# Short matmuls sent one by one between the long ones in a planned Trainium2 kernel

## The chip, the cores and the metric

The kernel runs on one core of a Trainium2 chip. The metric is the device time of one execution in microseconds (us). A core has TensorE (PE; its weight loads are shown apart as PEld), VectorE (DVE), ScalarE (ACT), GpSimd (POOL) and the DMA queues that SyncE (SP) and GpSimd issue to. Each engine works through its own list of instructions in order, and engines wait for each other on semaphores.

## The reference

The input `A_x` has 2048 rows of 512 numbers. Two branches are computed from it and mixed by a gate for each row:

```python
def reference(A_x, A_w_r, A_w_i, B_x, B_w1, B_b1, B_w2, B_b2, gate_w):
    # X = rfft2(x); X = X * (w_r + 1j * w_i); a = irfft2(X)          (spectral filter)
    # b = gelu(x @ w1 + b1) @ w2 + b2                                 (512 -> 1792 -> 512)
    g = _sigmoid((x * gate_w).sum(-1, keepdims=True))
    a = _A_ref(x, A_w_r, A_w_i)
    b = _B_ref(x, B_w1, B_b1, B_w2, B_b2)
    return g * a + (1 - g) * b
```

Everything is in 32-bit floats. Both branches are given the same `x`.

## The kernel before

**Tiling.** The 2048 rows are 16 blocks of 128, and four groups (c = 0 to 3) of four blocks make the 512 columns of one matmul in the dense branch. Matmuls take operands rounded to a shorter mantissa, so each operand is split into a high and a low part and a product is made of three: high x high, high x low, low x high (`prods`, line 533).

**The dense branch** is `mlp(half, c)`: 14 slices of the hidden width in two halves, four groups each. For a slice, `up` (line 1087) makes the tile `ph` by twelve matmuls of 512 columns (four slices of the input, three products each); ACT applies the gelu, and `split` makes its high part on ACT and its low part on DVE (`g_...`). Then `down` adds three matmuls of 512 columns for each slice into the tiles `po`. The last `po` is made in two pieces of 256 columns.

**The spectral branch** has a forward part, `forward(j)`, for each of the 16 blocks: DVE folds the block, and the step at line 736 makes, for each of two products c, two matmuls of 260 columns from the high part (`pd<-cf,eoh`); the step at line 737 adds two of 130 columns from the low part (`pd<-cf,eol`). ACT (lines 739, 740) and DVE (742, 743) read `pd`, three matmuls of 512 columns make `py`, and ACT and DVE put it into `y`. Then come butterflies on `y` and the filter, all on DVE, and the way back, `inverse(c, h)`: for each of two blocks, `pz` is made by two matmuls of 256 columns from the high part (`some(vh, 0, True)`) and, in the step `rest` (line 971), two of 128 from the low part, two of 256 and again two of 128; ACT (line 979) and DVE (980) read `pz`. Twelve matmuls of 256 columns make `pa`.

**The order of the work** is not the order of the code. Each call of `m`, `a`, `v`, `dma` and so on adds a step to a graph (`Graph.add`), with an engine, a cost, a lag from its end until others may use its result, the buffers that it reads and writes, and a rank. `Graph.schedule` then plays the engines through: whenever one is free by its clock, it takes the ready step with the lowest rank for which buffers are free. Ranks come from the list `RANKS`, one number for each step. The plan's order is the order in which instructions are emitted, for all engines and DMA queues. For TensorE the cost is given by `c_pe` (line 495), with a floor for short matmuls:

```python
    def c_pe(n, k=1):
        return k * max(n / 2400 + 0.0135, 0.112)
```

that is, n columns at 2400 a microsecond and 0.0135 us, but not under 0.112 us, for each of k matmuls. All matmuls are issued by the helper `mm`, so they have line 531 in the profile and are told apart by tile.

Of the kernel before, what the change touches and what calls it, by code (L numbers as in the profile page):

```python
# [17 lines left out]
P = 128  # L18
NJ = S // P
NF = F // P  # L20
NQ = D // P
# [6 lines left out]
NC = P + 2  # L28
# [132 lines left out]
class Step:  # L161
    def __init__(self, n, eng, cost, lag, emit, bufs, rank):
        self.n, self.eng, self.cost, self.lag, self.emit, self.bufs, self.rank = n, eng, cost, lag, emit, bufs, rank
        self.after = []
        self.need = 0

        self.open = 0
        self.there = 0.0
        self.table = None
        self.at = None  # L170


class Graph:
# [47 lines left out]
    def schedule(self):  # L221
# [11 lines left out]
        wire = 0.0  # L233
        events = []
# [32 lines left out]
        while True:  # L267
            for e in list(ready):
                while ready[e] and busy.get(e, 0.0) <= now:
                    kept, got = [], None  # L270
                    while ready[e]:
                        r = heapq.heappop(ready[e])
                        new = takes(r[2])
                        if new is None or held(e, r[2]):
                            kept.append(r)
                            continue
                        got = r[2]
                        break
                    for r in kept:
                        heapq.heappush(ready[e], r)  # L280
                    if got is None:
                        break
                    s = got
                    for b in new:
                        b.slot = free[b.tag].pop(0)
                        held_by[b.cls] += 1
                        nxt[b.cls] += 1
# [6 lines left out]
                    if e in ("sp", "pool"):  # L294
                        busy[e] = now + (0.5 if e == "sp" else 0.95)
                        wire = max(wire, now) + s.cost
                        end = wire + s.lag
                    else:
                        busy[e] = now + cost
                        end = now + cost + s.lag  # L300
                    for q in s.after:
# [990 lines left out]
```

## Time and profile before

| what | value |
|---|---|
| median of 3 runs | 373.58 us (373.31 to 374.03) |
| the profiled execution's own time | 372.75 us |
| its span, first to last instruction | 370.6 us |
| granted TensorE clock | 0.999 |
| matmuls | 1790: 1370 of 512 columns, 292 of 256 to 260, 64 of 130, 64 of 128 |
| DVE busy | 326.6 us |
| ACT busy | 234.5 us |

The profile is of one execution. Its page has busy times by engine, the same by slices of the span, and the chain that ended last; other views give waits, groups of instructions by line or tile, busy time in stretches, and the instructions in order of time. In a timeline row the columns are the start in us, the length in us, the engine, the line, the operation, output tile <- input tiles, shapes, and how many were merged into the row ("x2"). Matmuls overlap in the array: the length of one runs from its entry to the end of its results, so two lengths cover the same time in part, and distances between starts say how fast TensorE goes. A matmul and its weight load are separate instructions; the load (PEld) of a matmul stands ahead of it.

### The profile page before, as it was taken

The numbers are of one execution on the slowest core, as the hardware profiler recorded it, in microseconds if no ns is written. First come the engines' busy times: TensorE is split into PE (matmuls) and PEld (weight loads), VectorE is DVE, ScalarE is ACT, GpSimd is POOL, SyncE is SP. The second block draws the span as 40 slices with busy tenths as digits, with TensorE's granted clock in tenths as the row PEclk, the third lists the DMA queues.
The fourth block names the chain that finished last, engine by engine and source line by source line (L and its number), as shares of the span: only waits on it lengthen the run. The fifth ranks groups of instructions, "written<-read, shape, count | busy, mean of one in ns | idle before, by whom it ended". The sixth has DMA issues, their size and how long they took to land.

```text
span 370.6 us, 5520 instructions
## 1 busy us (share of the span) xinstructions
PE 364.5 (98%) x1790; PEld 307.4 (83%) x1790; DVE 326.6 (88%) x689; ACT 234.5 (63%) x462; POOL 44.1 (12%) x54
## 2 busy tenths in 40 slices
PE   7999999999999999999999999999999999999995
PEld 6888888888888888888888788888888888888895
DVE  5999889999999779899998999878749895989996
ACT  6768697886679655355366313697497649647820
POOL 0000000000000002021023011000332123111041
PEclk9999999999999999999999999999999999999999
DMA  8952889324953205587489792308996999824368
GB/s 278 381 184 72 287 297 356 105 86 145 309 167 112 84 22 146 144 197 172 140 191 243 130 259 42 73 0 309 183 142 124 182 286 239 142 73 99 114 88 197
DMA packets 39628, 62.99 MB, mean 170 GB/s; under 512 B 4656, under 2 KB 17008, under 8 KB 38832
## 3 DMA queue, kind: packets, MB, share of 16 engines
q1 hardware_dynamic: 32256, 49.54, 40.6%
q0 software_dynamic: 7200, 12.85, 23.7%
q8 instruction: 14, 0.23, 0.3%
q10 hardware_dynamic: 144, 0.26, 0.2%
q14 instruction: 14, 0.11, 0.1%
HBM read 38.64 MB, written 23.73 MB: 168 GB/s over the span
## 4 chain that ended last, share of the span: by engine, by line
PE 76%; DVE 14%; DMA 6%; issue 2%; ACT 1%; SPq 0%
PE ph L531 32%; PE po L531 31%; DMA wf<-in_wf 5%; PE pz L531 4%; PE pd L531 4%; PE pa L531 3%; PE py L531 3%; DVE m L911 2%; DMA xr<-in_xt 1%; DVE y L811 1%; DVE y L813 1%; DVE y L815 1%; ACT mxh L655 0%; DVE y L915 0%; DVE y L913 0%
## 5 line engine op out<-in xcount | busy, mean ns | idle before, releaser
L1108 ACT ACTIVATE ph<-ph,b1t 128x512 f32<-128x512 f32 x56 | 36.8, 658 | 55.2 <-PE ph L531 55.1
L952 ACT ACTIVATE sw<-y,al 64x512 f32<-64x512 f32 x32 | 22.9, 721 | 3.1 <-DVE y L815 2.0
L959 DVE SCALAR_TENSOR_TENSOR pq<-y,al,sw 128x256 f32<-128x256 f32 x32 | 14.3, 481 | 8.5 <-ACT sw L955 7.8
L911 DVE TENSOR_TENSOR m<-y,wf 128x514 f32<-128x514 f32 x32 | 20.9, 690 | 0.2
L522 POOL DMA_DIRECT2D bacc<-o x12 | 11.2, 972 | 64.7 <-ACT o L1157 64.7
L522 POOL DMA_DIRECT2D wa7l<-in_w x1 | 1.0, 1015 | 142.9 <-ACT wa7l L583 142.9
L1154 ACT ACTIVATE o<-po,b2t 128x512 f32<-128x512 f32 x16 | 10.8, 687 | 9.1 <-PE po L531 9.1
L765 ACT ACTIVATE y<-py 64x256 f32<-64x256 f32 x32 | 12.1, 379 | 3.7 <-PE py L531 3.1
L1157 ACT ACTIVATE o<-po 128x512 f32<-128x512 f32 x12 | 6.9, 594 | 10.5 <-PE po L531 10.5
L531 PEld LDWEIGHTS pd<-cf,eoh 128*128 128x128 f32 x64 | 10.9, 188 | 2.1 <-ACT eoh L710 0.5
L1005 DVE TENSOR_TENSOR uv<-pa,od 128x512 f32<-128x512 f32 x16 | 10.5, 686 | 2.3 <-ACT od L1002 2.1
L531 PE MATMUL pd<-cf,eoh 128*128 128x260 f32 x64 | 12.4, 288 | 0.1
L762 ACT ACTIVATE y<-py 64x256 f32<-64x256 f32 x32 | 12.1, 378 | 0.5
L694 DVE TENSOR_TENSOR eo<-xr 128x256 f32<-128x256 f32 x30 | 11.7, 420 | 0.0
L1049 DVE SCALAR_TENSOR_TENSOR ba<-gb,ba 128x512 f32<-128x512 f32 x12 | 8.3, 688 | 2.8 <-DMA ba<-bacc 2.7
L531 PE MATMUL pd<-cf,eol 128*128 128x130 f32 x64 | 10.5, 251 | 0.0
L531 PEld LDWEIGHTS pd<-cf,eol 128*128 128x128 f32 x64 | 10.0, 188 | 0.3
L1002 ACT ACTIVATE od<-pa 128x512 f32<-128x512 f32 x8 | 4.8, 598 | 8.5 <-PE pa L531 8.5
L955 ACT ACTIVATE sw<-y 1x512 f32<-1x512 f32 x16 | 10.0, 628 | 0.3
L708 DVE TENSOR_TENSOR xr<-eo 128x256 f32<-128x256 f32 x24 | 9.7, 421 | 0.2
L522 POOL DMA_DIRECT2D out<-ba x8 | 7.3, 909 | 20.6 <-DVE ba L1049 10.3
L655 ACT ACTIVATE mxh<-xm 128x512 fp32r<-128x512 f32 x12 | 7.1, 629 | 3.6 <-PE ph L531 3.6
(713 smaller groups left out, 1337.3 us busy)
## 6 DMA issues: line engine op xcount, KB each, us to landing
wf<-in_wf SPq DMA_DIRECT2D x16, 257.0 KB, 3.7
bacc<-o SPq DMA_DIRECT2D x16, 256.0 KB, 4.7
xr<-in_xt SPq DMA_DIRECT2D x15, 256.0 KB, 4.1
war<-in_w SPq DMA_DIRECT2D x14, 256.0 KB, 3.9
wbr<-in_w SPq DMA_DIRECT2D x14, 256.0 KB, 4.1
xm<-in_xt SPq DMA_DIRECT2D x12, 256.0 KB, 4.9
bacc<-o POOLq DMA_DIRECT2D x12, 256.0 KB, 4.5
ba<-bacc SPq DMA_DIRECT2D x12, 256.0 KB, 4.0
```

The lines of the kernel that those rows point to most:

```text
L522: return add("pool", kb / 150, 3.4, lambda: nc.gpsimd.dma_start(dst(), src(), accum_op=ALU.add), reads, writes, rank)
L531: pe.matmul(ps, w, x, start=start, stop=stop)
L694: v(lambda s=s, op=op: vec.tensor_tensor(eo.ap()[:, s], x.ap()[:, 0:2], x.ap()[:, 2:4], op=op), 256, [x], [(eo, s)], FEED)
L762: a(lambda o=o, i=i: act.activation(apart(0, o, HP), py.ap()[i:i + HP, 1].rearrange("p (a b) -> p a b", a=2), AF.Copy), HD, [py], [(Y[j], ...
L765: a(lambda o=o, i=i: act.activation(Y[j].ap()[o:o + HP, 1, :HD], py.ap()[i:i + HP, 0], AF.Copy, scale=-1.0), HD, [py], [(Y[j], 1 + k)], 0, ...
L911: v(lambda mk=mk, k=k, y=y, w=w: vec.tensor_tensor(mk.ap(), y.ap()[:, :, :ND], w.ap()[:, k:k + 1, :ND].to_broadcast([P, 2, ND]), op=ALU.mu ...
L952: a(lambda sw=sw, y=y, o=o, i=i: act.activation(sw.ap()[o:o + HP], y.ap()[i:i + HP, ::-1, :HD], AF.Copy, scale=al.ap()[i:i + HP, 0:1]), 51 ...
L955: a(lambda sw=sw, y=y, j=j: act.activation(sw.ap()[HP:HP + 1], y.ap()[HP:HP + 1, ::-1, :HD], AF.Copy, scale=math.cos(math.pi * j / NJ)), 5 ...
L959: v(lambda sw=sw, pq_=pq_, y=y, j=j, k=k, op=op: vec.scalar_tensor_tensor(pq_.ap()[:, k], y.ap()[:, k, :HD], al.ap()[:, 1 + j:2 + j], sw.a ...
L1005: v(lambda i=i, op=op: vec.tensor_tensor(uv.ap()[:, :, i], ps.ap()[:, 0], od.ap(), op=op), 512, [ps, od], [(uv, i)], 2)
L1108: a(lambda f=f, ps=ps: act.activation(ps.ap(), ps.ap(), AF.Gelu_apprx_tanh, bias=b1t.ap()[:, f:f + 1]), 600, [b1t], [ps], 0.9 if half else ...
L1154: a(lambda o=o, ps=ps, q=q: act.activation(o.ap(), ps.ap(), AF.Identity, scale=-1.0, bias=b2t.ap()[:, q:q + 1]), 600, [b2t, ps], [o])
```

## The change

Steps of at most 130 columns (the low parts of `pd` and `pz`) are marked "short", those of 512 columns "long". When the plan is turned into instructions, the matmuls of a short step are held back. If the next step on TensorE is long, its matmuls and the held ones are issued in turn: one held, one long, one held, one long, and the rest of the long ones. Held ones are issued by themselves when a step of any engine is due at or after the time at which the plan counts their result as there, or when the next TensorE step is neither short nor long. The planner takes, after a short step, a ready long one ahead of lower ranks. It counts a short matmul without the floor, and the lag of a short step is longer by the cost of one long matmul for each matmul after the first. `up` becomes four steps of three matmuls, and the second step of `pz` three steps of two. There are 2040 ranks in place of 1843, all of them new. The matmuls themselves are the same.

```diff
@@ Graph.schedule
-                    kept, got = [], None
-                    while ready[e]:
-                        r = heapq.heappop(ready[e])
-                        new = takes(r[2])
...
+                    got = None
+                    for kind in ("long", None) if e == "pe" and last == "short" else (None,):
+                        kept = []
+                        while ready[e]:
+                            r = heapq.heappop(ready[e])
+                            if kind and r[2].kind != kind:
+                                kept.append(r)
+                                continue
+                            new = takes(r[2])
+                            if new is None or held(e, r[2]):
+                                kept.append(r)
+                                continue
+                            got = r[2]
+                            break
...
                     s = got
+                    if e == "pe":
+                        last = s.kind
...
+                    s.end = end
@@ tile_kernel
     def c_pe(n, k=1):
-        return k * max(n / 2400 + 0.0135, 0.112)
+        return k * (n / 2400 + 0.0135)
...
     def m(emit, n, k, reads, writes, rank=BULK):
-        return add("pe", c_pe(n, k), 0.25, emit, reads, writes, rank)
+        if n > P + 2:
+            s = add("pe", c_pe(n, k), 0.25, emit, reads, writes, rank)
+            s.kind = "long" if n == 4 * P else None
+        else:
+            s = add("pe", k * (n / 2400 + 0.0135), 0.25 + (k - 1) * c_pe(4 * P), emit, reads, writes, rank)
+            s.kind = "short"
+        return s
...
+    now = []
+
     def mm(ps, w, x, start, stop):
-        pe.matmul(ps, w, x, start=start, stop=stop)
+        now.append(lambda: pe.matmul(ps, w, x, start=start, stop=stop))
@@ forward
-            m(lambda c=c: prod(c, l, NC, False), 240, 2, [l, *cf_of(c)], [pd[c]], 0)
+            m(lambda c=c: prod(c, l, NC, False), NC, 2, [l, *cf_of(c)], [pd[c]], 0)
@@ inverse
             m(lambda some=some, vh=vh: some(vh, 0, True), 256, 2, [t, vh], [ps], FEED)
-            m(rest, 256, 6, [t, vh, vl], [ps], FEED)
+            m(lambda some=some, vl=vl: some(vl, 0, False), P, 2, [t, vl], [ps], FEED)
+            m(lambda some=some, vh=vh: some(vh, 1, True), 256, 2, [t, vh], [ps], FEED)
+            m(lambda some=some, vl=vl: some(vl, 1, False), P, 2, [t, vl], [ps], FEED)
@@ mlp
-                m(up, 512, 12, [*W["a", f], *xx], [ps])
+                for q in range(NQ):
+                    m(lambda up=up, q=q: up(q), 512, 3, [*W["a", f], *xx], [ps])
@@ the end of tile_kernel
     with tc.manual_schedule():
+        held = []
+        until = 0.0
+
+        def flush(between):
+            out = []
+            for k in range(max(len(held), len(between))):
+                out += held[k:k + 1] + between[k:k + 1]
+            for f in out:
+                f()
+            held.clear()
+
         for s in order:
+            if held and (s.at >= until or s.eng == "pe" and s.kind is None):
+                flush([])
+            now.clear()
             s.emit()
+            if s.kind == "short":
+                held += now
+                until = min(until, s.end) if len(held) > len(now) else s.end
+            elif now:
+                flush(list(now))
+        flush([])
```

More of the change, by code (lines that the diff above doesn't have):

```diff
@@ L170, in __init__ @@
         self.at = None
+        self.end = None
+        self.kind = None
 class Graph:
@@ L233, in schedule @@
         wire = 0.0
+        last = None
         events = []
@@ L269, in schedule @@
                 while ready[e] and busy.get(e, 0.0) <= now:
-                    kept, got = [], None
-                    while ready[e]:
-                        r = heapq.heappop(ready[e])
-                        new = takes(r[2])
[L274 to L280, printed above, removed]
+                    got = None
[12 more added lines that the diff above has]
+                            break
+                        for r in kept:
+                            heapq.heappush(ready[e], r)
+                        if got:
+                            break
                     if got is None:
@@ L969, in some @@
                     mm(ps.ap()[:, ft, k, :n], x.ap()[:, k, ft * P:(ft + 1) * P], t.ap().rearrange("p a b -> p (a b)")[:, :n], first, not first)
-            def rest(some=some, vh=vh, vl=vl):
-                some(vl, 0, False)
-                some(vh, 1, True)
-                some(vl, 1, False)
             m(lambda some=some, vh=vh: some(vh, 0, True), 256, 2, [t, vh], [ps], FEED)
-            m(rest, 256, 6, [t, vh, vl], [ps], FEED)
+            m(lambda some=some, vl=vl: some(vl, 0, False), P, 2, [t, vl], [ps], FEED)
+            m(lambda some=some, vh=vh: some(vh, 1, True), 256, 2, [t, vh], [ps], FEED)
+            m(lambda some=some, vl=vl: some(vl, 1, False), P, 2, [t, vl], [ps], FEED)
             a(lambda n=n, ps=ps: act.activation(zh.ap()[:, :, :, n], ps.ap()[:, :, :, :P], AF.Copy), 512, [ps], [(zh, n)])
@@ L1085, in mlp, with up @@
             ps = buf("pm", [P, 512], F32, f"ph{c}_{f}", pool=pp, cls="ph", parts=2)
-            def up(f=f, ps=ps):
+            def up(q, f=f, ps=ps):
                 wh, wl = (t.ap() for t in W["a", f])
                 xh, xl = (t.ap() for t in xx)
-                for q in range(NQ):
-                    s = slice(q * P, (q + 1) * P)
-                    prods(ps.ap().rearrange("p (a b) -> p a b", b=P), wh[:, s], wl[:, s], xh[:, :, q], xl[:, :, q], q == 0, q == NQ - 1)
+                s = slice(q * P, (q + 1) * P)
+                prods(ps.ap().rearrange("p (a b) -> p a b", b=P), wh[:, s], wl[:, s], xh[:, :, q], xl[:, :, q], q == 0, q == NQ - 1)
             if half == c == f == 0:
```

228 rows, old and new, of the table RANKS are left out of this document.

## The prediction

> **What bounds the kernel now.** I read the page's busy table and chain of waits first, then the busy time by stage, then the waits of TensorE's two parts, and last the timeline around the matmuls that the change moves.
>
> ```profile
> span 370.6 us, 5520 instructions
> PE 364.5 (98%) x1790; PEld 307.4 (83%) x1790; DVE 326.6 (88%) x689; ACT 234.5 (63%) x462; POOL 44.1 (12%) x54
> PEclk9999999999999999999999999999999999999999
> PE 76%; DVE 14%; DMA 6%; issue 2%; ACT 1%; SPq 0%
> ```
>
> ```profile
> 20.00:110.00 90.00, 89.92 (x456) 75.98 (x455) 85.01 (x200) 69.00 (x178) 0.00 (x0) 1.00 0.60 196
> ```
>
> ```profile
> PEld ph L531 <- ACT mxh L655: 1.4, 2, 0.9
> ...
> PEld ph L531 <- DVE g_11l L578: 0.5, 1, 0.5
> PEld pd L531 <- ACT eoh L710: 0.5, 1, 0.5
> ```
>
> TensorE is busy for 364.5 of 370.6 us at the full clock, and it has 76% of the chain. The columns of the stage row are the length, then PE, weight loads, DVE and ACT: from 20 to 110 us, where the forward transforms run, TensorE lacks 0.08 us and VectorE 5.0 us of being full. TensorE's weight loads wait for data for 1.4 us at the head and for 0.5 us twice later on; the rest is matmuls that follow each other. So a new order can win almost nothing by itself. It has to make the matmuls closer, and the question is what a short matmul (128 or 130 columns) costs, and whether that cost changes when its neighbours do.
>
> **Prices.** A matmul's duration in these views includes its way through the array, so I price by the distance between starts.
>
> ```profile
> 126.58 2.72 PE ph L531 x12
> ```
>
> ```profile
> 363.77 0.28 PE L531 MATMUL po<-g_9h,wb9l 128*128 128x256 f32 x1
> ...
> 366.29 0.28 PE L531 MATMUL po<-g_13h,wb13l 128*128 128x256 f32 x1
> ```
>
> ```profile
> 282.65 0.64 PE L531 MATMUL pa<-z00h,ci 128*128 128x256 f32 x4
> ...
> 284.51 0.39 PE L531 MATMUL ph<-mxh,wa11h 128*128 128x512 f32 x1
> ```
>
> ```profile
> 322.80 0.40 PE L531 MATMUL pz<-tg,v10h 128*128 128x256 f32 x2
> 323.03 0.34 PE L531 MATMUL pz<-tg,v10l 128*128 128x128 f32 x2
> ...
> 324.42 0.34 PE L531 MATMUL pz<-tg,v14l 128*128 128x128 f32 x2
> 324.60 0.45 PE L531 MATMUL po<-g_9h,wb9h 128*128 128x512 f32 x1
> ...
> 326.03 0.39 PE L531 MATMUL ph<-mxh,wa10h 128*128 128x512 f32 x1
> ```
>
> The first row is a stretch of the chain: 12 matmuls of 512 columns in 2.72 us, 0.227 each. The next two rows lie 21 matmuls of 256 columns apart: 2.52/21 = 0.120 each. Between 282.65 and 284.51 stand four of 256 and six of 512 columns, 1.86 us; the plain sum is 4 x 0.120 + 6 x 0.227 = 1.84, so going back to a stream of 512 costs another 0.02. Between 322.80 and 326.03 stand eight of 256, eight of 128 and six of 512 columns: 3.23 - 0.96 - 1.36 - 0.02 = 0.89, or 0.111 for a short one. From the first two prices a column costs (0.227 - 0.120)/256 = 0.00042 us, so 128 columns by themselves would be 0.120 - 0.053 = 0.067. The difference, 0.045 us, is what there is to win on each short matmul.
>
> ```profile
> L531 PE MATMUL pd<-cf,eol 128*128 128x130 f32 x64 | 10.5, 251 | 0.0
> ```
>
> ```profile
> 245.00:360.00 115.00, 16.65 (x128) 16.77 (x128) 21.68 (x32) 9.54 (x16) 1.00 0.73 158
> ```
>
> There are 64 of 130 columns (pd) and, in the row for pz, 128 matmuls of which half are short by the code: 128 in all, 128 x 0.045 = 5.8 us at the very most.
>
> **Why they cost 0.111, and what holding them back does to that.**
>
> ```profile
> 166.15 0.39 PE L531 MATMUL ph<-mxh,wa5h 128*128 128x512 f32 x1
> 166.15 0.19 PEld L531 LDWEIGHTS ph<-mxl,wa5h 128*128 128x128 f32 x1
> 166.38 0.39 PE L531 MATMUL ph<-mxl,wa5h 128*128 128x512 f32 x1
> ```
>
> ```profile
> 32.02 0.34 PE L531 MATMUL pd<-cf,eol 128*128 128x130 f32 x2
> ...
> 32.13 0.19 PEld L531 LDWEIGHTS py<-x0l,tf 128*128 128x128 f32 x1
> 32.19 0.44 PE L531 MATMUL py<-x0l,tf 128*128 128x512 f32 x1
> 32.24 0.42 PEld L531 LDWEIGHTS pd<-cf,eol 128*128 128x128 f32 x2
> ...
> 32.47 0.33 PE L531 MATMUL pd<-cf,eol 128*128 128x130 f32 x2
> ```
>
> In the steady stream the load for a matmul starts with the matmul just before it, never a matmul earlier: at 166.15 the load for the one at 166.38. So TensorE loads one ahead. In the second fence a load begins 0.11 after the one before it (32.13, 32.24), so a load keeps its path for 0.11 us. A short matmul streams for 0.067 and the load behind it takes 0.11: the remainder, 0.045, is waited for by the matmul *after* the short one. In the fence the 512-column matmul at 32.19 is stamped 0.06 after its load, and yet the next matmul is 0.28 away and not 0.23: it took the 0.05 on itself. The whole of it, two short and one long from 32.02 to 32.47, is 0.45 - 0.227 = 0.223, again 0.111 for each short.
>
> Now the change, which sends short, long, short, long. The short one's own load lies under the long matmul before it, but that was not what it paid for. The load of the long one after it can start only with the short one, lasts 0.11, and is again 0.045 too long. Each short matmul pays as before: 128 x (0.111 - 0.111) = 0. No row shows a short matmul alone between two long ones; the bounds are 0.067 (full cover, 5.8 us less) and 0.111, and I take 0.111 because both halves of it, the load's start and its 0.11, are in rows. [...]
>
> **The rest, part by part.** *Pairs taken apart.* Now short pairs often run on into the next 256- or 260-column matmul:
>
> ```profile
> 41.91 0.34 PE L531 MATMUL pd<-cf,eol 128*128 128x130 f32 x2
> 42.08 0.45 PE L531 MATMUL pd<-cf,eoh 128*128 128x260 f32 x2
> ...
> 356.51 0.34 PE L531 MATMUL pz<-tg,v13l 128*128 128x128 f32 x2
> ```
>
> These are the first and the last of 24 such places in the timeline. With the change a long step stands there, so 24 more returns to the 512 stream: 24 x 0.02 = +0.5 us. At best the returns run into each other (0); if each of the 128 gets its own, against the 40 pairs that have one now, it is 88 x 0.02 = +1.8. I take +0.5.
>
> *The up-projection in four steps of three matmuls instead of one of twelve, and the inverse's second step in three.* The same 1790 matmuls; only the planner sees finer pieces: 0. *The planner's price.* Its floor of 0.112 goes, so it plans shorts at 0.067 and TensorE falls behind its plan by 128 x 0.045 = 5.8 us in all, half of it in the forward stage. What TensorE waits for then comes early rather than late; ACT and DVE wait for TensorE, and the 5.0 us that DVE has free in that stage cover the 2.9. No cost; without that cover, rival B.
>
> *New order on every queue.* All ranks are new, so SP's and POOL's DMAs are dealt out anew too, with none added. What a better order can take away are the two waits of 0.5: -1.0. What a worse one brings no row bounds; I put the same +1.0 against it and take 0. *Waits.* None is added, but the second short matmul of a held pair now stands behind a long one, and if that waits for its operands, so do the short one and the ACT copies of pd and pz with DVE's subtractions behind them. *Head and tail* stay: the last matmul starts at 366.29, 4.3 us before the end.
>
> **Sum.** 0 (shorts) + 0.5 (returns) + 0 (order) = +0.5 us on the profiled execution of 372.75 (span 370.6 and 2.15 around it): 373.25. The median of the runs, 373.58, is 0.83 above that execution, so the forecast is 373.25 + 0.83 = 374.1. Its own range is -1.0 to +1.8 around 373.6, or 372.6 to 375.4. About 0.2% (0.75 us, 372.8 to 374.3) is what a measurement of this kernel can tell from no change.
>
> **Rivals.** *A, the loads are hidden after all.* If a load could be drawn ahead of two matmuls, the long one's load would also lie under the long matmul before the short one, and each short cost 0.067: 373.6 - 5.8 = 367.8. For it speaks that before a short matmul the long one leaves 0.227 - 0.11 = 0.12 us of the load path empty, just enough for a second load. Against it: at 166.15 that room is there and no second load uses it. [...]
>
> *B, slower: the spectra come too late.* Place: the forward stage, 20 to 110 us. The planner now puts a long step after each short one, so in each of 16 blocks the second product's results can land six long matmuls later, 6 x 0.227 = 1.36 us; 16 x 1.36 = 21.8. DVE works on those results (x, y) and also makes the low parts that TensorE's own long steps need. It decides from the point where DVE loses more than the 5.0 us it has free, 0.31 a block. If a third of the delay is not filled, 7.3 are lost, 2.3 of them felt by TensorE: 374.1 + 2.3 = 376.4. Against it: the planner knows of the delay (it is in the step's lag), and ACT has 21 of 90 us free.
>
> *C, the change hardly does what it says.* A held matmul is sent plain when another engine's step is due or a 256-column step comes next. If most go that way, the matmuls' neighbours stay as they are: 373.6.
>
> **How the numbers follow.** Forecast 0.65, A 0.11, B 0.17, C 0.07. The forecast's range puts 0.05 of its chance below 372.8, 0.38 within and 0.22 above. Faster: 0.05 + A 0.11 + C 0.01 = 0.17. Same: 0.38 + C 0.06 = 0.44. Slower: 0.22 + B 0.17 = 0.39. The range reaches from 372.0 (the forecast's low end less a tenth of A's 5.8) to 376.6 (B and a spread of 0.2); A and the far part of B are left out.
>
> **What would show it.** Right: in the timeline after, a load for the long matmul starts with the short one before it, and that long one is followed at 0.28; short plus long is 0.34 from start to start. The loads after short matmuls would still be 0.11 apart, and PE would stay within 1 us of 364.5 busy. Rival A: 0.29 for the two, and a span about 6 us shorter. Rival B: PE waits in the stage row from 20 to 110 that grow by more than 2 us, on ACT or DVE. Rival C: short matmuls still in twos. The forecast is wrong if a load starts earlier than the matmul before its own, or if TensorE's idle time changes by more than 1 us.

## The result, and the profile after

The changed kernel takes 375.44 us (median of 8 runs, 374.83 to 376.76) and the kernel before, in the same series, 373.44 us (8 runs, 372.05 to 374.03). The ratio is 1.0062, with a 95% interval of 1.0042 to 1.0082: slower by 0.6%, 2.0 us by the medians. That is inside the range of 372.0 to 376.6, but at the very end of the forecast's own part of it (372.6 to 375.4) and not where its likeliest case lay (374.1, within 0.2%).

The profiled execution after took 375.19 us, its span 373.3 us. In this kernel `mm` is line 564. The first lines are from its page, the next from the busy time by stage (columns: length, then PE, weight loads, DVE and ACT), the last from the waits of TensorE's weight loads.

```profile
span 373.3 us, 5512 instructions
PE 364.8 (98%) x1790; PEld 307.2 (82%) x1790; DVE 326.8 (88%) x689; ACT 235.2 (63%) x462; POOL 44.1 (12%) x54
PE 94%; DVE 2%; DMA 1%; ACT 1%; issue 0%; SPq 0%
```

```profile
20.00:110.00 90.00, 90.00 (x455) 75.90 (x455) 83.66 (x200) 67.57 (x176) 0.00 (x0) 1.00 0.63 197
```

```profile
PEld ph L564 <- ACT mxh L688: 2.2, 2, 1.5
PEld none L564 <- DVE zero L631: 1.1, 1, 1.1
PEld pa L564 <- ACT z10h L1009: 0.9, 1, 0.9
```

TensorE is as busy as before (364.8 against 364.5), and in the forward stage it lacks nothing at all. The two waits of 0.5 us are gone, and one of 0.9, for the inverse's `z10h`, is new. So neither a large gain nor starvation. But the span has grown by 2.7 us, so TensorE's idle time went from 6.1 to 8.5 us. The next lines are the timeline where two short matmuls are sent between long ones.

```profile
349.35 0.22 PE L564 MATMUL pz<-tg,v5l 128*128 128x128 f32 x1
349.35 0.19 PEld L564 LDWEIGHTS po<-g_12h,wb12h 128*128 128x128 f32 x1
349.40 0.46 PE L564 MATMUL po<-g_12h,wb12h 128*128 128x512 f32 x1
349.46 0.19 PEld L564 LDWEIGHTS pz<-tg,v5l 128*128 128x128 f32 x1
...
349.70 0.22 PE L564 MATMUL pz<-tg,v5l 128*128 128x128 f32 x1
```

This is the picture that the prediction drew. The long matmul's load starts with the short matmul (349.35) and not earlier; the next load follows 0.11 later (349.46); and from one short matmul to the next, with one long between, it is 0.35 us. With 0.227 for the long one the short one has cost 0.12, not 0.067. Of the 128 short matmuls, 119 now stand between others with a 512-column one behind them, so the change does what it says; 69 of these have a 512-column one in front too, and the other 50 come straight after one of 256 or 260 columns.

Where the 2.7 us between the two profiled spans lie is read from four rows of the timeline after and three of before: the first matmul of 512 columns behind the head, the last two of the last `pa`, the last matmul of all, and the last instruction of DVE.

```profile
10.06 0.40 PE L564 MATMUL ph<-mxh,wa1h 128*128 128x512 f32 x1
...
363.84 0.40 PE L564 MATMUL pa<-z11l,ci 128*128 128x256 f32 x2
...
367.56 0.28 PE L564 MATMUL po<-g_13h,wb13l 128*128 128x256 f32 x1
...
369.76 0.42 DVE L1205 TENSOR_TENSOR o<-y,o 128x256 f32<-128x256 f32 x1
```

```profile
9.67 0.40 PE L531 MATMUL ph<-mxh,wa1h 128*128 128x512 f32 x1
...
361.13 0.40 PE L531 MATMUL pa<-z11l,ci 128*128 128x256 f32 x2
...
367.26 0.42 DVE L1175 TENSOR_TENSOR o<-y,o 128x256 f32<-128x256 f32 x1
```

The head is 0.39 longer (10.06 against 9.67); TensorE's weight loads wait there 2.2 us for `mxh`, made from the first inputs, against 1.4 before, and the same changed kernel had 9.65 in another execution, so I don't count it to the change. From there to the last matmul, which was at 366.29, TensorE takes 357.50 instead of 356.62: +0.88. And from the last matmul to the end of the span it is 5.74 instead of 4.31: +1.43. The tail is longer because of what stands in front of it. The row of the last `pa` starts at 363.84 and the span ends 9.46 later; before it was 361.13 and 9.47. The last `pa` moved by 2.71 = 0.39 + 0.88 + 1.44, the last term being twelve matmuls of 256 columns (0.12 each) that used to follow it and now stand ahead: it is the 31st matmul from the end instead of the 43rd.

The chain that ended last is not the same in the two. After, it runs through ACT's copy of the last `pa` into DVE's last steps. Before, it runs through the matmuls that TensorE does behind that `pa`:

```profile
361.54 3.97 PE po L531 x33
365.51 0.02 issue
365.53 0.42 DVE o L1170
```

There, too, DVE works almost without a break from the last `pa` on (its first step on that `pa` starts at 362.20, its last instruction ends at 367.68). So before the change the two chains met at 365.5, to a few hundredths of a microsecond.

How far the end moved is cleaner by DVE's last instruction than by the span, because behind it the trace has nothing but the last output's DMA, and the span ended 2.6 to 4.0 us behind it in the profiles of this document. Counted from the first 512-column matmul, DVE's last instruction ends at 358.01 before and at 360.12 after: 2.1 us later.

### The profile page after: what moved, and what is told of

It is laid out like the page before. It is cut to its first block, busy times and chain, and to the rows that moved or that the text cites. A ratio compares the mean times of both kernels' runs of the same rounds, so it can differ in the third digit from the quotient of the medians.

```text
span 373.3 us, 5512 instructions
## 1 busy us (share of the span) xinstructions
PE 364.8 (98%) x1790; PEld 307.2 (82%) x1790; DVE 326.8 (88%) x689; ACT 235.2 (63%) x462; POOL 44.1 (12%) x54
## 4 chain that ended last, share of the span: by engine, by line
PE 94%; DVE 2%; DMA 1%; ACT 1%; issue 0%; SPq 0%
PE ph L564 41%; PE po L564 41%; PE py L564 3%; PE pd L564 3%; PE pa L564 3%; PE pz L564 3%; DMA xr<-in_xt 1%; DVE uv L1035 0%; DVE y L1057 0%; ACT mxh L688 0%; DVE y L1054 0%; SPq L1097 0%; DVE o L1205 0%; DVE z10l L1010 0%; DVE o L1200 0%
## 5 line engine op out<-in xcount | busy, mean ns | idle before, releaser
L564 PE MATMUL pd<-cf,eol 128*128 128x130 f32 x64 | 14.1, 223 | 0.0
L564 PEld LDWEIGHTS pd<-cf,eol 128*128 128x128 f32 x64 | 12.1, 190 | 0.3
L743 ACT ACTIVATE eoh<-xr 128x512 fp32r<-128x512 f32 x12 | 7.6, 630 | 3.9 <-PE pd L564 3.8
```

The lines of the kernel that those rows point to most:

```text
L564: now.append(lambda: pe.matmul(ps, w, x, start=start, stop=stop))
```

## The experiments

The theory was now: (1) a short matmul costs 0.11 in either place; what the change loses, it loses by its new order, mostly by the late last `pa`. The rivals: (2) sending them one by one costs the 2 us directly; (3) it does hide the loads, and the order lost even more.

**The short matmul by itself.** The kernel before with stretches of matmuls on zeros behind the warm-up, whose result nothing uses; `go(n)` issues one of n columns.

```diff
             mm(none.ap(), zero.ap(), bcast(zero.ap(), 4), True, True)
...
+        for reps, ns in ((30, (512,)), (30, (512, 128)), (15, (512, 512, 128, 128)), (30, (512,)), (30, (128,)), (30, (512,)),
+                         (30, (512, 64)), (30, (512,)), (30, (512, 256)), (10, (512, 512, 512, 512, 512, 512, 512, 512, 128)), (30, (512,))):
+            for _ in range(reps):
+                for n in ns:
+                    go(n)
```

> The kernel before with a run of matmuls on a tile of zeros put behind the warm-up, whose result nothing uses: stretches of 512 alone; 512 and 128 in turn; 512, 512, 128, 128; 128 alone; 512 and 64 in turn; 512 and 256 in turn; eight of 512 and one of 128. It costs the short matmul by itself. Theory 1 (each load starts with the matmul before its own and takes 0.11): 0.34 for a 512 and a 128, 0.68 for two and two, 0.11 for 128 alone, 0.34 also with 64 columns, 0.347 with 256. Rival 3 (a lone short one's follower has its load hidden): 0.294 for a 512 and a 128, 0.267 with 64.

The view is busy time by stretch for these matmuls alone, cut at the starts of the stretches; the columns are the length, PE with the number of matmuls that touch the stretch, the weight loads with theirs.

```profile
12.83:22.98 10.15, 10.15 (x61) 8.91 (x60) 1.00 0.38 144
22.98:33.27 10.29, 10.29 (x62) 8.98 (x61) 1.00 0.00 0
40.14:43.44 3.30, 3.30 (x32) 3.30 (x30) 1.00 0.02 5
50.34:60.52 10.18, 10.18 (x62) 8.90 (x60) 1.00 0.00 0
67.42:78.01 10.59, 10.59 (x61) 9.18 (x60) 1.00 0.00 0
78.01:97.47 19.46, 19.46 (x92) 16.09 (x91) 1.00 0.00 1
```

A 512 and a 128 in turn: 10.15/30 = 0.338. Two and two: 10.29/15 = 0.686, or 0.343 for one of each. 128 alone: 3.30/30 = 0.110. With 64 columns: 10.18/30 = 0.339, the same as with 128. With 256: 0.353. Eight of 512 and one of 128: 1.946, so the lone short one costs 1.946 - 8 x 0.227 = 0.13, which is 0.11 and one return of 0.02. Everything is within 0.01 of what theory 1 had, and rival 3 (0.294, and 0.267 with 64) falls: half the columns are no cheaper. That it is the load behind that is paid for is read from the start times. A fixed least time of 0.11 us for any matmul would give the same sums; against it stands only that the long matmul starts 0.05 behind the short one and is then itself longer (0.46 against 0.39 us). No run has a short matmul without a load behind it.

**Only the 130-column ones held, in the plan of before.**

```diff
     def m(emit, n, k, reads, writes, rank=BULK):
-        return add("pe", c_pe(n, k), 0.25, emit, reads, writes, rank)
+        s = add("pe", c_pe(n, k), 0.25, emit, reads, writes, rank)
+        s.kind = {512: "long", 240: "short"}.get(n)
+        return s
...
```

What is left out are the lines that hold the matmuls back and send them, the same as in the change.

> The kernel before, its plan unchanged, with only the 64 matmuls of 130 columns (pd) held back and sent between the long ones wherever a long step comes next; 52 of them then stand alone between two longer ones. Theory 1: no gain, 0 to 0.5 us slower than before. Rival 2: 52 of 119 lone ones bring a like part of the change's 2 us, about 0.9 us slower. Rival 3 (loads hidden): 52 x 0.045 = 2.3 us faster.

Measured: 373.86 against 373.47 us, ratio 1.0020 (1.0005 to 1.0034). No gain from 52 lone matmuls, and a loss of 0.2 to 1.3 us; the expected 0 to 0.5 and rival 2's 0.9 both lie in that. Rival 3 (2.3 faster) falls again.

```profile
10.15 0.40 PE L538 MATMUL ph<-mxh,wa1h 128*128 128x512 f32 x1
...
367.06 0.28 PE L538 MATMUL po<-g_13h,wb13l 128*128 128x256 f32 x1
```

From the first 512-column matmul to the last matmul of all it is 356.91 us, 0.29 more than before. In this order a 512-column matmul comes after a shorter one 81 times instead of 53, so 28 more returns cost about 0.01 each.

**The plan of the change without the interleaving.** Nothing is held, all steps are in the change's order.

```diff
...
         for s in order:
-            if held and (s.at >= until or s.eng == "pe" and s.kind is None):
-                flush([])
             now.clear()
             s.emit()
-            if s.kind == "short":
-                held += now
-                until = min(until, s.end) if len(held) > len(now) else s.end
-            elif now:
-                flush(list(now))
-        flush([])
+            for f in now:
+                f()
```

> The plan of the changed kernel, the same order of steps on every engine, but a short step's matmuls are issued in place, next to each other, and none is held back. Theory 1 (a short matmul costs 0.11 us in either place, and the change's loss is in its new order): within 0.5 us of the changed kernel, so 1 to 2.5 us slower than before; the last product of the inverse (pa) stands at the same place, 31 matmuls from the end, and the span ends 9.1 us after it. Rival 2 (sending them one by one is itself what costs, through more returns to the 512-column stream): 1.5 to 2 us faster than the changed kernel, level with before. Rival 3 (the loads are hidden when sent one by one, and the new order lost more than that won): about 5 us slower than the changed kernel.

Measured: 374.95 us, ratio to before 1.0048 (1.0030 to 1.0067), so 0.5 us from the change, as theory 1 had it. Rival 2 by itself (level with before) falls, and so does rival 3 (5 us slower than the change). The expected 9.1 us behind the last `pa` did not come out: it is 10.4.

```profile
span 373.3 us, 5513 instructions
9.81 0.40 PE L564 MATMUL ph<-mxh,wa1h 128*128 128x512 f32 x1
...
362.89 0.40 PE L564 MATMUL pa<-z11l,ci 128*128 128x256 f32 x2
...
366.61 0.28 PE L564 MATMUL po<-g_13h,wb13l 128*128 128x256 f32 x1
...
368.81 0.43 DVE L1205 TENSOR_TENSOR o<-y,o 128x256 f32<-128x256 f32 x1
```

The span is as long as the change's, though the last matmul is 0.7 earlier. The difference lies behind DVE's last instruction: 4.0 us to the end of the span, against 3.1 in the change. DVE's last instruction ends at 359.43 after the first 512-column matmul; that is 1.4 later than before and 0.7 earlier than with interleaving.

This run was timed on another chip than the change, so both were run once more on one chip.

> The changed kernel once more, on one chip beside its plan without interleaving (next run), since the two were timed on different chips before. Theory 1: 1.5 to 2.5 us slower than before, and 0.3 to 0.9 us slower than the next run, which is what the records of TensorE show for the interleaving (0.7 us more between its matmuls).

> The changed kernel's plan with short matmuls next to each other, beside the run above. Theory 1: 1 to 2 us slower than before and 0.3 to 0.9 us faster than with interleaving. Rival 2 (interleaving is the whole loss): level with before.

Measured: with interleaving 375.44, ratio 1.0066 (1.0053 to 1.0079); without 374.07, ratio 1.0033 (1.0019 to 1.0047). The expected 0.3 to 0.9 between the two became 1.2 by the ratios. Theory 1 has to share: the new order costs 1.2 to 1.8 us (0.0033 here, 0.0048 in the first timing) and the interleaving 1.2 to 0.5 (0.0033 and 0.0014). In the records of the plan without interleaving the stretch from the first 512-column matmul to the last matmul is 356.80, so 0.70 of the change's 357.50 comes from the interleaving and 0.18 from the order. TensorE stands still once in that stretch in both, for 0.6 us ahead of a `pa` that needs `z10h`. What differs is the number of times a 512-column matmul comes after a shorter one: 53 before, 81 in the new order, 140 with interleaving. So 59 more returns cost 0.70, or 0.012 each. In the second pair the stretch was 358.65 and 356.79. The next lines are the last matmul and the waits of the weight loads in the second interleaved run.

```profile
368.30 0.28 PE L564 MATMUL po<-g_13h,wb13l 128*128 128x256 f32 x1
```

```profile
PEld ph L564 <- DVE g_8l L611: 1.0, 1, 1.0
PEld pa L564 <- ACT z10h L1009: 0.9, 1, 0.9
```

There TensorE also waited 1.0 us for a low part from DVE, which neither the plan without interleaving nor the first profile of the change shows. So part of the second pair's difference is this wait and not returns; what causes it and how often it comes is not shown.

**The last pa made late in the kernel before.** The planner alone is told that the last block's `pz` comes later.

```diff
-            m(rest, 256, 6, [t, vh, vl], [ps], FEED)
+            add("pe", c_pe(256, 6), 0.25 + (1.36 if (c, h) == (1, 1) else 0.0), rest, [t, vh, vl], [ps], FEED)
```

> The kernel before, with nothing held. Only the planner is told that the last inverse block's pz (c = 1, h = 1) is there 1.36 us later, six long matmuls, so that it plans the copies and the pa behind it later; the last pa then stands 22 matmuls from the end instead of 43. Theory 1 (the end is set by the chain of ACT, DVE and DMA behind the last pa, 9.1 us long in both kernels): 21 x 0.12 = 2.5 us slower than before. Rival (TensorE's work sets the end, where the last pa stands does not matter): no change.

Measured: 375.52 us, ratio 1.0058 (1.0035 to 1.0082), so 2.2 us slower.

```profile
span 372.8 us, 5520 instructions
```

```profile
363.48 0.40 PE L531 MATMUL pa<-z11l,ci 128*128 128x256 f32 x2
...
364.56 0.69 DVE L1005 TENSOR_TENSOR uv<-pa,od 128x512 f32<-128x512 f32 x1 [1.97 <-ACT od L1002]
...
366.12 0.28 PE L531 MATMUL po<-g_13h,wb13l 128*128 128x256 f32 x1
```

Its last matmul comes at 366.12, even 0.17 earlier than before, and the span is 2.2 longer: the last `pa` is 2.35 later (363.48 against 361.13), and 9.3 behind it the span ends. DVE stood idle for 1.97 us until ACT had copied this `pa`. The rival (TensorE's work sets the end) falls.

**Six matmuls moved past the last pa.** In the change's plan six matmuls of 256 columns stand between the two steps of the last `pa`. They go behind it, with and without interleaving (the edit below; `first` and `second` mark the two steps of that `pa`, `end` the ones with 256 columns); and in the kernel before, six that follow it go between.

```diff
...
     order = g.schedule()
+    i, k = (next(n for n, s in enumerate(order) if s.mark == w) for w in ("first", "second"))
+    moved = [s for s in order[i:k] if s.mark == "end"]
...
+    order = [*order[:i], *(s for s in order[i:k] if s.mark != "end"), order[k], *moved, *order[k + 1:]]
```

> The changed kernel, plan and all, except for one spot on TensorE: the six matmuls of 256 columns (po) that stand between the two steps of the last pa go behind it. The last pa is then 6 x 0.12 = 0.72 us earlier (37 matmuls from the end instead of 31). Theory 1 (the chain behind the last pa sets the end): 0.5 to 0.75 us faster than the changed kernel. Rival (TensorE's work sets the end): no change.

> The same swap in the changed kernel's plan without interleaving (short matmuls next to each other). Theory 1: 0.5 to 0.75 us faster than that plan without the swap (374.95), and 0.4 to 0.6 us faster than the swap with interleaving. Rival: no change from 374.95.

> The kernel before with the opposite swap: six matmuls of 256 columns (po) that follow the last pa go between its two steps, as the changed kernel has them, so the last pa is 0.72 us later (37 from the end instead of 43). Theory 1: 0.4 to 0.75 us slower than before. Rival: no change.

Measured: 374.65 us for the change with the swap, ratio to before 1.0041 (1.0024 to 1.0059), down from 1.0062 and 1.0066; 374.75 without interleaving, 1.0032 (1.0013 to 1.0052), beside 1.0048 and 1.0033 for that plan without the swap; 373.60 for the opposite swap in the kernel before, whose runs there had 372.86, 1.0006 (0.9990 to 1.0022). (The ratios are taken over the whole series and differ from quotients of the medians: for the last the medians give 1.0020.) By the ratios the first is some 0.8 us down, as theory 1 had it, but its interval overlaps those without the swap, and they come from other chips. The second is not 0.4 to 0.6 faster than the first, as expected: by the medians the two are level. The third can't be told from no change nor from the expected loss. So the times decide nothing here. The profile of the first:

```profile
362.71 0.40 PE L565 MATMUL pa<-z11l,ci 128*128 128x256 f32 x2
...
363.15 0.60 ACT L1035 ACTIVATE od<-pa 128x512 f32<-128x512 f32 x1 [2.75 <-PE pa L565]
...
364.29 1.28 DVE L1038 TENSOR_TENSOR uv<-pa,od 128x512 f32<-128x512 f32 x2
...
367.15 0.28 PE L565 MATMUL po<-g_13h,wb13l 128*128 128x256 f32 x1
```

Its last matmul is at 357.50 after its first long one (9.65), exactly as in the change, so TensorE's work is the same; the `pa` is 4.44 ahead of it instead of 3.72, and the tail is 5.25 instead of 5.74. But most of that lies again behind DVE's last instruction. That one ends at 359.96 after the first long matmul, only 0.16 earlier than in the change: the copy of `pa` was done at 363.75, and DVE came to it at 364.29, because it still had earlier steps to do. Without interleaving the swap wins 0.2 in the same count.

So the last `pa` is not alone. In the change DVE has almost no gap from the last block's low part on (from 360.85 to its end it idles 0.25 us; before, from 357.98, 0.37 us). That low part waits for the last block's `pz`, and it came 1.6 us later than before in the new plan without interleaving and 2.5 later in the change, counted from the first long matmul. The kernel before with the opposite swap shows the other side: there the `pa` came late enough for DVE to wait for it.

```profile
363.48 1.29 DVE L1008 TENSOR_TENSOR uv<-pa,od 128x512 f32<-128x512 f32 x2 [0.77 <-ACT od L1005]
```

Its DVE ends at 358.91 in that count, 0.9 later than before.

**The plan nudged.** Three runs let the planner make a new order with ranks that were made for another: the last inverse group ranked earlier, with and without interleaving, and the measured price for short matmuls.

```diff
-        s.rank = r / 100
+        s.rank = r / 100 - (15 if s.early else 0.0)
```

Here `early` marks the steps of `back(1)`, the last inverse group.

```diff
-            s = add("pe", k * (n / 2400 + 0.0135), 0.25 + (k - 1) * c_pe(4 * P), emit, reads, writes, rank)
+            s = add("pe", k * 0.112, 0.25 + (k - 1) * c_pe(4 * P), emit, reads, writes, rank)
```

> The changed kernel with the ranks of all steps of the last inverse group (c = 1: its butterflies, pz, pa and what follows) lowered by 15, so that the planner takes them earlier; short matmuls are held as in the change, 113 of 128 stand alone. The last pa now stands 43 matmuls from the end, as before the change, instead of 31. Theory 1 (the change's loss is mostly that the last pa comes late): 1 to 1.5 us faster than the changed kernel, so 374.0 to 374.5, what is left being the half microsecond that sending one by one costs. Rival 2 (the loss is in the interleaving everywhere): level with the changed kernel.

> The same with nothing held back: short matmuls next to each other, in the same plan. Theory 1: another 0.5 us faster, 373.3 to 373.9, level with before. Rival 3 (lone short matmuls hide their loads): slower than the same plan with interleaving by some 5 us.

> The changed kernel, but the planner counts a short matmul at its measured 0.112 us again; ranks as in the change. The plan comes out otherwise: 94 lone short matmuls, and the last pa is the last matmul of all. Theory 1 (the chain behind the last pa sets the end, about 9 us): the span ends about 9 us after TensorE's last matmul instead of 4.3, so 4 to 5 us slower than before, although the plan's price is now right. Rival (the change lost because its planner has TensorE too fast): faster than the changed kernel.

Measured: 383.25 (ratio 1.0275, 1.0251 to 1.0299), 381.45 (1.0216, 1.0198 to 1.0235) and 406.12 us (1.0876, 1.0838 to 1.0915). All three expectations missed. The waits of TensorE in the first, and in the third its stage row and its longest waits, say why.

```profile
PE pa L565 <- ACT z10h L1010: 1.3, 1, 1.3
PE pz L565 <- DVE v5l L612: 1.2, 1, 1.2
```

```profile
20.00:110.00 90.00, 81.17 (x386) 66.76 (x385) 74.52 (x177) 56.67 (x148) 0.00 (x0) 0.94 0.51 162
```

```profile
PE pd L564 <- DVE x9l L776: 3.3, 1, 3.3
PE pd L564 <- DVE x5l L776: 2.5, 2, 1.5
```

The rows are waits of TensorE; the column behind the four engines and POOL in the stage row is the granted clock. In the first and the third TensorE waits for DVE and ACT, several times over a microsecond, and in all three the granted clock was lower: 0.94 in the third from 20 to 110 us, where TensorE was busy for 81.17 of 90, and 0.986 and 0.984 over the profiled executions of the first two, against 0.999 before. So these runs decide nothing about the price or the tail; only that in the third the span ends 8.6 us after a `pa` that is the last matmul of all (393.24 and 401.8) fits theory 1. Between the first two, the interleaved one is the slower again. No run beat the kernel before.

## Why the prediction was right and wrong

**The price of a short matmul: right.** "Each short matmul pays as before: 128 x (0.111 - 0.111) = 0." The change's rows give 0.12 with the return in it, the stretches on zeros 0.11, and rival A (367.8 us) is out. In the rows after, the long matmul is stamped 0.05 us behind the start of its load (349.40 against 349.35), whose own length is 0.19, and that wins no time: on zeros a long and a short one in turn took 0.338. Loads are one ahead here too: in the traces before and after, none of the 1790 weight loads starts before the matmul just ahead of its own.

**The returns: right in kind, counted wrong.** I had 24 more returns of 0.02 each, +0.5, with an upper end of 88 and 1.8. There are 87 more, 28 of them from the new order and 59 from the interleaving, and they cost about 0.012 each: 0.70 for the interleaving in the first pair. In times, interleaving cost 0.5 to 1.2 us in the two pairs. That the sum was not further off is luck: the count was too low and the price too high.

**The order: the step that failed.** "What a worse one brings no row bounds; I put the same +1.0 against it and take 0", and "Head and tail stay: the last matmul starts at 366.29, 4.3 us before the end". The order cost 1.2 to 1.8 us (ratios 1.0033 and 1.0048 with nothing interleaved), and nearly all of it is in the tail: from the last matmul's start to the end of DVE's last instruction it is 1.4 us before and 2.6 in the new order, with and without interleaving. I had read the tail as a constant behind the last matmul. It is the longest of chains that end together: one behind the last matmul, and one from the last inverse block's `pz` over its copies and the last `pa` through DVE's last steps. Before the change the 42 matmuls after that `pa` (5.04 us to the last one's start) just covered the second. A plan that brings that block later pays, as the kernel with only its `pa` late showed (2.2 us for 2.35). Which link of that chain is the last to come is not the same in every plan: there DVE waited for the `pa`, and in the change moving the `pa` 0.72 us forward brought DVE's end only 0.16 forward.

**A sign of being wrong came true.** The prediction named itself wrong "if TensorE's idle time changes by more than 1 us". It grew by 2.4 us, by 1.4 of them in the tail and 0.4 in the head. That the measured time came out at the end of the forecast's own part of the range is in part luck: its +1.8 was worked out from returns alone, and over half of the loss was in the tail.

**Rival B: the mechanism in part, the place wrong.** Products do land later, but they cost nothing in the forward stage, where TensorE was busy for 90.00 of 90 us and DVE had 6.3 us free. They show in the inverse, at the end of the kernel. The next rows are one block's `pz`, after and before.

```profile
358.21 0.39 PE L564 MATMUL pz<-tg,v13h 128*128 128x256 f32 x2
...
359.96 0.22 PE L564 MATMUL pz<-tg,v13l 128*128 128x128 f32 x1
```

```profile
356.27 0.40 PE L531 MATMUL pz<-tg,v13h 128*128 128x256 f32 x2
...
357.14 0.45 PE L531 MATMUL po<-g_10h,wb10h 128*128 128x512 f32 x1
```

Eight matmuls that were through in 0.87 us now take 1.75 from the first to the start of the last, with long ones between. The plan without interleaving has the late `pa` too, at the same place from the end, so the sending in turn is not its cause. Whether it comes of the planner putting long steps behind short ones, of the wrong price in the plan or simply of other ranks stays open: the runs that would have parted them needed ranks of their own.

**Other points.** Rival C is out (119 of 128). That the plan's lower price costs nothing was not tested cleanly. The forecast's likeliest case was too small by 1.3 us, and its odds (0.44 same, 0.39 slower) leaned to the wrong side.

## What to carry to other kernels

In this kernel each matmul brings its own weights (1790 loads for 1790 matmuls) and its load starts no earlier than the matmul just ahead of it (349.35 in the rows after), and a short one cost about the shortest distance between two loads (0.11 us): 0.110 in a row of its own, 0.12 between long ones, 0.13 behind eight of them. Before re-sorting matmuls, look when the load *after* the short one starts. Count how often the stream changes its width under the new order, not only at the places that the change aims at. In a kernel whose main engine is full, find every chain that ends with the last instruction and how much the longest leads, because here 1.2 of the 1.4 us that the new order alone cost by DVE's last instruction lay there. Measure the end by the last instruction of an engine as well as by the span: here what lay behind it varied from 2.6 to 4.0 us. A list of ranks belongs to one plan: the three runs that changed the planner's rules or ranks lost 8 to 33 us here, so such a run says little before it has ranks of its own.

## What the runs showed of the hardware

A matmul of 64 columns between 512-column ones costs the same as one of 128 (0.339 and 0.338 for the pair). A 256-column one in the same place costs 0.353 - 0.227 = 0.126, a little over its 0.120 in a row of its own. A lone short matmul after eight long ones costs 0.13 (1.946 for the nine, less 8 x 0.227), of which 0.02 is about the return to the stream that I had seen after a run of 256 (282.65 to 284.51). In the changed kernel, where a 512-column matmul comes after a shorter one 140 times, I estimate a return at less, about 0.012: 0.70 us for 59 more of them than without interleaving.
